# A RetNet recurrence with a low-rank mixer on one core: three pieces of the hand-written order moved

## The chip, the core and the metric

The kernel runs on one core of a Trainium2 chip. A core has five engines that work through their own queues in order and meet through semaphores: PE (matrix products; PEld is its weight load), DVE (vector), ACT (scalar activations and copies), POOL (GpSimd) and SP (which here only issues DMAs). PE writes its results to PSUM, which has eight banks of 128 partitions x 2 KB; DVE and ACT read them from there into SBUF, the working memory. The metric is the device time of one execution in microseconds (us), as the median of several runs. All times inside an execution are counted from the start of the profiled span.

## The reference

```python
def _attn_ref(q, k, v):                        # 4 batches, 8 heads, 768 steps, 64
    gamma = 1.0 - 2.0 ** (-5.0 - np.arange(H)); scale = 1.0 / np.sqrt(D)
    for t in range(S):
        state = gamma * state + np.einsum('bhd,bhe->bhde', k[:, :, t], v[:, :, t])
        y[:, :, t] = scale * np.einsum('bhd,bhde->bhe', q[:, :, t], state)

def _moe_ref(x, U, V, w_ch1, w_ch2):           # x: 4 x 768 x 512, rank 32, hidden 2048
    h = x.transpose(0, 2, 1) @ U @ V
    u = x + h.transpose(0, 2, 1)
    ch = np.maximum(u @ w_ch1, 0.0) @ w_ch2
    return u + ch
```

The heads' outputs y are laid side by side as x (768 x 512 for each batch). A low-rank mix over the 768 steps makes u from x; a two-layer perceptron with a relu is added to it.

## The kernel before

**Stages.** The recurrence is computed in chunks of 128 steps, six for each batch. For a chunk `ci`, `state` (L482) adds the product of the chunk's k and v to a running state in PSUM bank `st` (L490) and has ACT copy it out (L498); `score` (L501) multiplies k with q (L506); `screen` (L510) has DVE multiply the two score banks with the causal mask (L516), giving `a0` and `a1`; `mix` (L532) forms the chunk's x from the state (L540) and from `a0` and then `a1` with v (L545) in bank `o`, which ACT copies out. q and k have to be turned first. In batch 1 that is done on PE (`turn_pe`, L461: four or eight 128x128 transposes, L465, into bank `qk`), with ACT copying the bank out, q in another order of columns (`q_order`, L453). In batches 2 and 3 DMA transposes do it (L475), and DVE reorders q (L87).

**From x to u.** `lr_proj` (L559) multiplies x with U into bank `o` (L563) and DVE copies the result `pc`. `lr_grow` (L571) multiplies `pc` with V (L576); the 512 columns are spread over four banks, in the order s, s, o and a last one, which is st here. `lr_add` (L580) has DVE add one of these banks to x, in place (L582). This is "plain u": rows are steps. `lr_turn` (L599) then turns u by DMA into `uT` for the perceptron. In batch 1, uT is made on PE instead (`x_turn`, `grow_turned`), and plain u comes later, when the perceptron of batch 1 already runs, since it is needed only for the final sums.

**The perceptron.** `mlp_pieces(b)` lists the pieces of batch b: 32 `up` pieces of four products (L763; 16 of 512 columns, 16 of 256), each emptied by ACT (L773) or DVE (L771) with a relu into `gT`; then the second layer. For batch 0 that is six output rows of 16 products of 512 columns in pieces of four (`down`, L814), each row ended by a DVE sum (L819). For batches 1 to 3 a seven-product scheme is used on 2x2 blocks (`down_pairs`, L643): each of the 21 pieces p1 to p7 of blocks 0 to 2 is a chain of eight products of 256 columns (L655) into banks called A (two of them), B and C. Several pieces add into one bank in turn, and between them DVE reads the bank: `keep` (L665) makes the sums `da`, `db`, `dc` (L668), `give` (L674) parts of the output rows (L676). The next piece on that bank has to wait for the read. `order` (L747) is the list of pieces. The scheme needs sums of the weights (`w2_sums`, L623) and of `gT` (`g_sums`, L633), all DVE instructions of line L608.

**What sets the order.** The program is in the order in which Python emits it; there is no scheduler. `weave` (L828) walks through the perceptron's pieces of batch b-1 and puts the recurrence of batch b between them. Each track is a list of steps with a start and an end as fractions of the pieces' summed cost; a step is emitted ahead of the first piece that begins at or after its mark. So a mark moves a step only in whole pieces, and steps with marks between the same two pieces are emitted in order of their marks. All five engines' queues follow from it: what a step issues to DVE stands ahead of everything that later steps issue to DVE, whether it is ready or not.

**The marks of this change.** In the block for b = 1 (perceptron of batch 0), `at` (L948) and `lag` place the steps of the six chunks; `more` and `late_by` (L1004, L1005) shift the score and the mix of each. L958 to L963 place the transposes, L970 to L973 the twelve weight sums. In the block for b = 2 (perceptron of batch 1), L984 to L986 place the growth and the four adds of batch 1's plain u; `two` (L978) places pairs of chunks, L1009 the last two mixes of batch 2. `t` (L1022) and the offsets at L1033 to L1041 place the projection, growth, adds and turns of batches 2 and 3.

PSUM banks are given out by `bank` from rings (L69): mlp has banks 0 to 2 (and bank 6 as a fourth from b = 2 on), s 3 and 4, o 5, qk 6, st 7, A 6 and 0, B 1, C 2. Whoever takes a bank again waits until its last reader is done.

Of the kernel before, what the change touches and what calls it, by code (L numbers as in the profile page):

```python
# [18 lines left out]
def kernel(  # L19
# [19 lines left out]
    NCB = DM // P  # L39
# [71 lines left out]
    def pair(b, sc):  # L111
        i = 2 * sc
        qs = [("q", b, sc, hh) for hh in range(2)]
        if b == 1:
            return [("k", b, i), *qs, ("v", b, i), ("k", b, i + 1),
                    ("v", b, i + 1)]
        return [("k", b, i), ("k", b, i + 1), *qs, ("v", b, i),
                ("v", b, i + 1)]
# [131 lines left out]
    for i in range(NST):  # L250
        t = consts.tile([P, 4, P], bf16, name=f"state{i}")
# [201 lines left out]
    def q_order(b, sc, src):  # L453
        t = rmid.tile([P, 2, 4, P], bf16, tag="qO", bufs=2, name=f"qO_{b}_{sc}")
        dst = t.rearrange("p x n (m two) -> p two n x m", two=2)
        src = src.rearrange("p two n (x m) -> p two n x m", x=2)
        for two in range(2):
            evac("A" if b == 1 else "D", dst[:, two], src[:, two])
        live["qO", b, sc] = t
# [147 lines left out]
    def part(f, *args, **kw):  # L607
        return lambda: f(*args, **kw)  # L608
# [14 lines left out]
    def w2_sums(m):  # L623
        r = ds(m, 2)
        lo, hi = w2b[:, r], w2b[:, ds(m + NH, 2)]
        b11, b12, b21, b22 = (lo[..., :DQ], lo[..., DQ:], hi[..., :DQ],
                              hi[..., DQ:])
        t1, t2, t3, t4 = (t[:, r] for t in w2t)
        return [part(nc.vector.tensor_tensor, o, x, y, ALU.subtract)
                for o, x, y in ((t1, b12, b11), (t2, b22, t1),  # L630
                                (t3, b22, b12), (t4, b21, t2))]
# [303 lines left out]
    for b in range(1, B + 1):  # L935
        tracks = []
        if b > 1:
            old = b - 1 < SEVEN
            first = [part(lr_expand, b - 1, 4, 2, "qk" if old else "st"),
                     part(lr_turn_pe, b - 1, 4, "qk" if old else "o")  # L940
                     if b < 3 else part(lr_turn, b - 1, 4)]
            if not old:
                RINGS["mlp"] = [6, 0, 1, 2]
        tracks.append((first, *((0.02, 0.2), (0.02, 0.14), (0.0, 0.06),
                                (0.0, 0.03))[b - 1]))
        if b < B:
            if b == 1:
                at = [0.503, 0.61, 0.675, 0.735, 0.793, 0.845]  # L948
                lag = [0.01, 0.035, 0.065]
                for sc in range(NSC):  # L950
                    keys = pair(b, sc)
                    c0, c1 = 2 * sc, 2 * sc + 1
                    if sc:
                        tracks.append(([part(prep_keys, b, keys[:AHEAD])],
                                       at[c0] - 0.1, 1))
                    tracks.append(([part(prep_keys, b, keys[AHEAD:])],
                                   at[c1] - 0.1, 1))
                    for f, d in ((part(turn_pe, "q", b, sc),  # L958
                                  at[c0] + (0.015, -0.042, -0.042)[sc]),
                                 (part(turn_pe, "k", b, sc, (0,)),  # L960
                                  at[c0]),
                                 (part(turn_pe, "k", b, sc, (1,)), at[c1])):
                        tracks.append(([f], d, d))  # L963
                for sc in range(NSC):
                    tracks.append(([part(prep_keys, 2, pair(2, sc))],
                                   0.752 + 0.03 * sc, 1))
                for i in range(2 * NSC):
                    tracks.append(([part(turn_dma, "kq"[i % 2], 2, i // 2)],
                                   0.84, 0.84))
                for f, d in zip(w2_sums(0) + w2_sums(2) + w2_sums(4),  # L970
                                (0.515, 0.535, 0.575, 0.6, 0.655, 0.67, 0.72,
                                 0.735, 0.78, 0.8, 0.875, 0.895)):
                    tracks.append(([f], d, d))  # L973
            else:
                at = [(0.205, 0.06)[b - 2] + (0.074, 0.1)[b - 2] * i
                      for i in range(NCK)]
                lag = [0.0, 0.04, 0.1]
                two = [(0.25, 0.395, 0.595), (0.1, 0.27, 0.44)][b - 2]  # L978
                if b == 2:
                    for _ in range(RING):  # L980
                        feed_one(False)
                    steps = [(0.01 + 0.022 * i, f)
                             for i, f in enumerate(w2_sums(6))]
                    steps.append((0.125, part(lr_grow, 1, 0, 4, "st")))  # L984
                    steps += [(0.125 + 0.022 * c, part(lr_add, 1, 0, 4, (c,)))
                              for c in range(NCB)]  # L986
                    for sc in range(NSC):
                        steps.append((0.57 + 0.08 * sc,
                                      part(prep_keys, 3, pair(3, sc))))
                        for nm in "kq":  # L990
                            if not sc:
                                steps.append((0.64, part(turn_dma, nm, 3, sc)))
                else:
                    steps = [(0.08, part(turn_dma, nm, 3, sc))
                             for sc in (1, 2) for nm in "kq"]
                for d, f in steps:
                    tracks.append(([f], d, d))
            if b > 1:
                for sc in range(NSC):
                    d = two[sc] - (0.04, 0.05, 0.08 if b == 2 else 0.05)[sc]  # L1000
                    tracks.append(([lambda b=b, sc=sc: q_order(
                        b, sc, live["q", b, sc])], d, d))
            for i in range(NCK):
                more = (0.012, 0.0, 0.0, 0.0, 0.0, -0.015)[i]  # L1004
                late_by = (0.015, 0.0, 0.012, 0.0, 0.01, 0.0)[i]  # L1005
                if b == 2 and i > 3:
                    p = two[2] + 0.05 * (i - 4)
                    steps = [(state, p - 0.035), (score_one, p),
                             (mix, p + (0.075, 0.067)[i - 4])]  # L1009
                elif b > 1:  # L1010
                    p = two[i // 2]
                    steps = [(state, p + (-0.035, 0.02)[i % 2]),
                             (mix, p + (0.08, 0.12)[i % 2])]
                    if i % 2 == 0:
                        steps.append((score_two, p))
                else:
                    steps = [(state, at[i] + lag[0]),
                             (score_one, at[i] + lag[1] + more),
                             (mix, at[i] + lag[2] + late_by)]
                for f, d in steps:  # L1020
                    tracks.append(([part(f, b, i)], d, d))
            t = at[-1] + lag[2] if b == 1 else two[-1] + 0.122  # L1022
            if b == 1:
                turns = [part(x_turn, c, j0, b, tag)
                         for c, tag in enumerate(("qk", "st", "s", "s"))
                         for j0 in (0, 2)]
                for fs, d in ((turns[:4], t + 0.006),
                              ([part(lr_open, b), part(lr_proj, b)], t + 0.022),
                              (turns[4:], t + 0.023),
                              ([part(grow_turned, b)], t + 0.044)):  # L1030
                    tracks.append((fs, d, d))
            else:
                for fs, d in (([part(lr_open, b), part(lr_proj, b)],  # L1033
                                0.025),
                              ([part(lr_grow, b, 0, 4, "st")], 0.047),
                              ([part(lr_add, b, 0, 4, (0,))], 0.047),
                              ([part(lr_add, b, 0, 4, (1,))], 0.057),
                              ([part(lr_add, b, 0, 4, (2,))], 0.082),
                              ([part(lr_add, b, 0, 4, (3,))], 0.102),
                              ([part(lr_turn, b, 0)], 0.107),  # L1040
                              ([part(lr_turn, b, 2)], 0.108)):  # L1041
                    tracks.append((fs, t + d, t + d))
        weave(b == 1, mlp_pieces(b - 1), *tracks)

# [28 lines left out]
```

## Time and profile before

| | |
|---|---|
| median of 7 runs | 221.83 us (221.64 to 222.46) |
| the profiled execution | 222.58 us |
| its span, first to last instruction | 220.8 us |
| granted PE clock | 1.000 |
| ACT L773, 98 relu evacuations | 47.4 us busy |
| DVE L771, 30 relu evacuations | 16.7 us busy |
| DVE L516, 128x512 masks | 682 ns each |
| PE L763, 512 products | 88.6 us busy |
| PE L655, chains of eight 256-column products | 273 ns for one product, pipelined |

The times of a PE instruction overlap: a product's duration runs until its result has left the array, and the next one begins earlier. So PE's pace is read from start to start. In the timeline, each line is: start, time in us, engine, line, operation, output<-inputs, shape, how many instructions are merged, and in brackets how long the engine had been idle and what it then waited for.

The stretches that matter here: from 51 to 59 us the first chunk of batch 1 runs between the last `up` pieces and the first `down` pieces of batch 0; from 84 to 96 us the perceptron of batch 1 starts and batch 1's plain u is made; from 116 to 127 us the last chunk of batch 2 and its u are made among the p pieces of batch 1.

### The profile page before, as it was taken

How to read it: one execution, taken by the hardware profiler on the slowest of the kernel's cores; microseconds unless marked ns; L12 is line 12 of the kernel's file. 1: busy time of each engine (PE TensorE's matmuls, PEld its weight loads, DVE VectorE, ACT ScalarE, POOL GpSimd, SP SyncE). 2: the span in 40 equal slices, each digit the busy share in tenths (PEclk: the TensorE clock that was granted, in tenths of full speed). 3: DMA queues.
4: the chain of work that ended last, by engine and by line, in shares of the span. 5: the costliest groups of instructions: out<-in, count | busy, mean ns of one | idle time of the engine just before them, and what ended most of it. 6: DMA issues, size and time to landing. Idle time of an engine off the chain costs nothing. (4 is left out here: it accounts for less than half of the span.)

```text
span 220.8 us, 5521 instructions
## 1 busy us (share of the span) xinstructions
PE 212.9 (96%) x2239; PEld 148.0 (67%) x2239; DVE 143.0 (65%) x303; ACT 92.8 (42%) x192; POOL 81.5 (37%) x121
## 2 busy tenths in 40 slices
PE   7979999999999999999999999999999999999994
PEld 2668754486456554567788784767788856668884
DVE  7487764433648748698785846598986442867443
ACT  3337845457355514667822005768510035551000
POOL 5439698897787957000049930000000000000000
PEclk9999999999999999999999999999999999999999
DMA  5999999999999999999999467900006341000043
GB/s 171 300 293 301 290 355 275 348 354 243 232 225 221 247 221 204 139 339 249 237 227 185 167 144 187 149 0 4 0 3 145 119 143 23 3 1 0 11 158 119
DMA packets 84489, 38.82 MB, mean 176 GB/s; under 512 B 58384, under 2 KB 77552, under 8 KB 84464
## 3 DMA queue, kind: packets, MB, share of 16 engines
q1 hardware_dynamic: 83456, 36.84, 69.8%
q10 hardware_dynamic: 1008, 1.64, 2.0%
q8 instruction: 17, 0.28, 0.5%
q14 instruction: 8, 0.07, 0.1%
HBM read 27.46 MB, written 6.29 MB: 153 GB/s over the span
## 5 line engine op out<-in xcount | busy, mean ns | idle before, releaser
L763 PE MATMUL mlp<-uT,w1b 128*128 128x512 f16 (+1 forms) x512 | 88.6, 326 | 0.0
L773 ACT ACTIVATE gT<-mlp 128x512 f16<-128x512 f32 (+1 forms) x98 | 47.4, 490 | 63.4 <-PE mlp L763 61.2
L763 PEld LDWEIGHTS <-w1b 128*128 128x128 f16 x512 | 48.2, 98 | 30.0 <-POOL w1b L340 0.2
L771 DVE TENSOR_SCALAR gT<-mlp 128x512 f16<-128x512 f32 (+1 forms) x30 | 16.7, 556 | 25.7 <-PE mlp L763 25.3
L655 PEld LDWEIGHTS <-gT 128*128 128x128 f16 x288 | 27.7, 98 | 3.3
L814 PE MATMUL mlp<-w2b,gT 128*128 128x512 f16 x96 | 23.6, 380 | 0.0
L516 DVE TENSOR_TENSOR a<-s,mask 128x512 bf16<-128x512 f32 x26 | 16.7, 682 | 10.0 <-PE s L506 10.0
L306 POOL TENSOR_TENSOR kd<-in,gk 128x512 bf16<-128x512 f32 x18 | 19.3, 1083 | 6.4 <-DMA in<-in_k_dram 6.3
L655 PEld LDWEIGHTS <-gS 128*128 128x128 f16 x200 | 19.2, 98 | 3.1 <-issue 0.5
L306 POOL TENSOR_TENSOR qd<-in,gq 128x512 bf16<-128x512 f32 x18 | 18.4, 1045 | 0.0
L655 PE MATMUL A<-w2t,gT 128*128 128x256 f16 x144 | 18.4, 273 | 0.0
L85 ACT ACTIVATE state<-st 64x256 bf16<-64x256 f32 x40 | 15.0, 374 | 6.7 <-PE st L386 3.2
L85 ACT ACTIVATE x<-o 128x512 f16<-128x512 f32 x20 | 11.9, 595 | 13.9 <-PE o L545 13.5
L814 PEld LDWEIGHTS <-gT 128*128 128x128 f16 x96 | 8.4, 98 | 8.1 <-issue 0.2
L304 POOL CAST vd<-in 128x512 bf16<-128x512 f32 x18 | 11.6, 662 | 1.6 <-DMA in<-in_v_dram 0.9
L346 POOL CAST w2b<-in 128x512 f16<-128x512 f32 x16 | 9.8, 616 | 1.5 <-DMA in<-in_moe_w_ch_dram 0.8
L608 POOL COPY gate<-gT 128x1 f16<-128x1 f16 x1 | 0.2, 190 | 26.5 <-DVE gT L608 26.5
L582 DVE TENSOR_TENSOR x<-s,x 128x256 f16<-128x256 f32 (+1 forms) x16 | 8.1, 548 | 2.7 <-PE st L576 1.5
L340 POOL CAST w1b<-in 128x512 f16<-128x512 f32 x16 | 9.2, 618 | 0.4 <-DMA in<-in_moe_w_ch_dram 0.2
L655 PE MATMUL B<-w2b,gT 128*128 128x256 f16 x72 | 9.3, 273 | 0.0
L655 PE MATMUL A<-w2t,gS 128*128 128x256 f16 x72 | 9.0, 273 | 0.3 <-DVE da L668 0.3
L655 PE MATMUL A<-w2b,gT 128*128 128x256 f16 x72 | 8.8, 273 | 0.0
(156 smaller groups left out, 292.8 us busy)
## 6 DMA issues: line engine op xcount, KB each, us to landing
in<-in_moe_w_ch_dram SPq DMA_DIRECT2D x32, 256.0 KB, 5.4
in<-in_k_dram SPq DMA_DIRECT2D x24, 256.0 KB, 5.4
in<-in_q_dram SPq DMA_DIRECT2D x24, 256.0 KB, 5.0
in<-in_v_dram SPq DMA_DIRECT2D x24, 256.0 KB, 5.4
out_dram<-o SPq DMA_DIRECT2D x16, 256.0 KB, 2.0
out_dram<-o ACTq DMA_DIRECT2D x6, 256.0 KB, 2.0
out_dram<-o SPq DMA_DIRECT2D x3, 128.0 KB, 1.7
Uf<-in_moe_U_dram SPq DMA_DIRECT2D x1, 96.0 KB, 5.4
```

The costliest lines, as they stand in the source:

```text
L85: nc.scalar.activation(dst, src, AF.Copy)
L304: nc.gpsimd.tensor_copy(out=t, in_=src)
L306: nc.gpsimd.tensor_tensor(t, src, g, op=ALU.mult)
L340: nc.gpsimd.tensor_copy(out=w1b[:, c, ts(mb, 512)], in_=take("w1", mb, c))
L346: nc.gpsimd.tensor_copy(out=w2b[:, m], in_=take("w2", m))
L516: nc.vector.tensor_tensor(a, four(sp[i]), causal(mask), op=ALU.mult)
L582: nc.vector.tensor_tensor(us[b][:, ds(j0, nj), ts(c, P)], four(grown[b][c])[:, :nj], xs[b][:, ds(j0, nj), ts(c, P)], op=ALU.add)
L655: nc.tensor.matmul(acc[key, i], lhs[:, m, ts(i, P)], rhs[:, m], start=(fresh and m == 0), stop=(m == NH - 1), skip_group_check=True)
L763: nc.tensor.matmul(g_p[:, :sz], w1b[:, c, ts(m, P)], uTs[b][:, ds(j, nj), c], start=(c == 0), stop=(c == NCB - 1))
L771: nc.vector.tensor_relu(gT[:, m, ds(lo, sz)], g_p[:, :sz])
L773: nc.scalar.activation(gT[:, m, ds(lo, sz)], g_p[:, :sz], AF.Relu)
L814: nc.tensor.matmul(ch, gT[:, m, ts(j, P)], w2b[:, m], start=(m == 0), stop=(m == NM - 1))
```

## The change

Only marks move, and the order of the four adds of batch 1.

```diff
@@ b == 1: transposes of q @@
                     for f, d in ((part(turn_pe, "q", b, sc),
-                                  at[c0] + (0.015, -0.042, -0.042)[sc]),
+                                  at[c0] + (0.035, -0.042, -0.042)[sc]),
@@ b == 1: weight sums @@
                 for f, d in zip(w2_sums(0) + w2_sums(2) + w2_sums(4),
-                                (0.515, 0.535, 0.575, 0.6, 0.655, 0.67, 0.72,
+                                (0.51, 0.525, 0.54, 0.585, 0.655, 0.67, 0.72,
                                  0.735, 0.78, 0.8, 0.875, 0.895)):
@@ b == 2: batch 1's plain u @@
                     steps.append((0.125, part(lr_grow, 1, 0, 4, "st")))
-                    steps += [(0.125 + 0.022 * c, part(lr_add, 1, 0, 4, (c,)))
-                              for c in range(NCB)]
+                    steps += [(0.125 + 0.022 * i, part(lr_add, 1, 0, 4, (c,)))
+                              for i, c in enumerate((3, 2, 0, 1))]
@@ the chunks' steps @@
-                more = (0.012, 0.0, 0.0, 0.0, 0.0, -0.015)[i]
-                late_by = (0.015, 0.0, 0.012, 0.0, 0.01, 0.0)[i]
+                more = (0.027, 0.0, 0.0, 0.0, 0.0, -0.015)[i]
+                late_by = (0.032, 0.0, 0.012, 0.0, 0.01, 0.0)[i]
                 if b == 2 and i > 3:
                     p = two[2] + 0.05 * (i - 4)
                     steps = [(state, p - 0.035), (score_one, p),
-                             (mix, p + (0.075, 0.067)[i - 4])]
+                             (mix, p + (0.07, 0.047)[i - 4])]
@@ the end of batches 2 and 3 @@
-            t = at[-1] + lag[2] if b == 1 else two[-1] + 0.122
+            t = at[-1] + lag[2] if b == 1 else two[-1] + (0.102, 0.122)[b - 2]
...
                               ([part(lr_add, b, 0, 4, (0,))], 0.047),
-                              ([part(lr_add, b, 0, 4, (1,))], 0.057),
-                              ([part(lr_add, b, 0, 4, (2,))], 0.082),
-                              ([part(lr_add, b, 0, 4, (3,))], 0.102),
-                              ([part(lr_turn, b, 0)], 0.107),
-                              ([part(lr_turn, b, 2)], 0.108)):
+                              ([part(lr_add, b, 0, 4, (1,))], 0.052),
+                              ([part(lr_add, b, 0, 4, (2,))], 0.066),
+                              ([part(lr_add, b, 0, 4, (3,))], 0.076),
+                              ([part(lr_turn, b, 0)], 0.08),
+                              ([part(lr_turn, b, 2)], 0.081)):
```

What the two programs' queues say, instruction by instruction:

- Chunk 0 of batch 1 on PE. Before: 4 products of output row 0, k transposes, state, q transposes, 8 products of row 0, scores, the last 4 of row 0, mix, 8 products of row 1. After: 4 of row 0, k transposes, state, 4 of row 0, q transposes, the last 8 of row 0, scores, 4 of row 1, mix, 4 of row 1. On DVE, the third weight sum and row 0's L819 come before the two masks and not behind them; the fourth weight sum stays behind.
- Batch 1's plain u on DVE. Before: banks s, s, a relu evacuation, o, st. After: st, o, the relu evacuation, s, s. PE's queue is the same.
- The end of batch 2 on PE. Before: p7 of block 1, p2 of block 1, mix of chunk 5, p4 of block 0, projection, p3 of block 0, growth, p4 of block 1. After: p7 of block 1, mix of chunk 5, p2 of block 1, projection, p4 of block 0, growth, p3 of block 0, p4 of block 1. On DVE, the adds of banks o and st come before the two reads of p4 and p5 of block 1 and not behind them, and the read of p3 of block 0 comes between the second and the third add.
- The end of batch 3: the marks change, and the order on every queue is as before. ACT, POOL and SP have the same order throughout.

## The prediction

> **What bounds the kernel now.** I read the page's busy times first, then who waited for whom on PE, then the timeline around each PE wait. All times are us from the span's start.
>
> ```profile
> PE 212.9 (96%) x2239; PEld 148.0 (67%) x2239; DVE 143.0 (65%) x303; ACT 92.8 (42%) x192; POOL 81.5 (37%) x121
> ```
>
> ```profile
> PE qk L465 <- ACT kT L85: 0.5, 1, 0.5
> ...
> PE st L490 <- DVE x L582: 0.3, 1, 0.3
> PE o L545 <- DVE a L516: 0.3, 1, 0.3
> PE A L655 <- DVE da L668: 0.3, 1, 0.3
> ```
>
> The first fence is the page's row of busy times, the second PE's waits (total, times, longest). PE is the bound, and the granted clock is full (1.000). After the start-up four single PE waits are left. Their idle figures count from a modelled end of the last matmul, so I measure by starts instead. PE's own pace, start to start, is 0.217 for a 128x512 product, 0.109 for a 128x256 one (eight: 0.87), 0.22 for four 128x128 and 0.23 for the eight 128x64 of a mix.
>
> ```profile
> 52.20 0.39 PE L465 MATMUL qk<-ident,kd 128*128 128x128 bf16 x4
> 52.43 0.39 PE L490 MATMUL st<-vd,kd 128*128 128x128 bf16 x4
> ...
> 52.63 0.60 ACT L85 ACTIVATE kT<-qk 128x512 bf16<-128x512 bf16 x1 [0.70 <-PE qk L465]
> ...
> 53.28 0.61 PE L465 MATMUL qk<-ident,qd 128*128 128x128 bf16 x8 [0.46 <-ACT kT L85]
> ...
> 55.54 0.40 PE L506 MATMUL s<-qO,kT 64*128 64x128 bf16 x8
> ...
> 55.97 1.29 DVE L516 TENSOR_TENSOR a<-s,mask 128x512 bf16<-128x512 f32 x2 [3.38 <-PE s L506]
> ...
> 57.18 0.68 DVE L819 TENSOR_TENSOR o<-mlp,x 128x512 f32<-128x512 f32 x1
> ...
> 57.32 0.29 PE L545 MATMUL o<-vd,a 128*128 128x64 bf16 x4 [0.29 <-DVE a L516]
> ```
>
> Chunk 0 of batch 1. After the L490 group (52.43+0.22=52.65) PE stands until ACT has emptied bank qk: 53.28, a gap of 0.63. The mix's first half starts at 56.74; its second half would follow 0.12 later, at 56.86, but the second mask is done at 57.26 and it starts at 57.32: 0.46.
>
> ```profile
> 90.45 1.29 DVE L582 TENSOR_TENSOR x<-s,x 128x512 f16<-128x512 f32 x2 [1.47 <-PE st L576]
> ...
> 93.50 0.68 DVE L582 TENSOR_TENSOR x<-st,x 128x512 f16<-128x512 f32 x1
> ...
> 94.32 0.38 PE L490 MATMUL st<-vd,kd 128*128 128x128 bf16 x4 [0.32 <-DVE x L582]
> ```
>
> Start of batch 2. The products begun at 90.35 (8 of 512, 16 of 256 columns: 3.48) are issued by 93.83; the state product waits for bank st, whose add is the fourth: gap 0.49.
>
> ```profile
> 123.13 1.28 DVE L582 TENSOR_TENSOR x<-s,x 128x512 f16<-128x512 f32 x2
> ...
> 125.92 0.68 DVE L582 TENSOR_TENSOR x<-st,x 128x512 f16<-128x512 f32 x1
> 126.52 0.41 DVE L668 TENSOR_TENSOR da<-A,x 128x256 f32<-128x256 f32 x1
> ...
> ...
> 126.98 1.03 PE L655 MATMUL A<-w2t,gS 128*128 128x256 f16 x8 [0.29 <-DVE da L668]
> ```
>
> End of batch 2. Two of batch 2's adds stand ahead of the sum da; p6 of block 2 goes on adding into that bank, so it waits: p2 began at 125.65, 0.87 later is 126.52, it starts at 126.98: 0.46. The four gaps make 2.04.
>
> **The change part by part.** No instruction is added or removed; pieces move. Lags I use, all from the timeline: 0.05 to 0.06 from an evacuation's end to the PE work it frees (53.23 to 53.28, 57.26 to 57.32); 0.43 from a score group's start to its first mask (55.54 to 55.97); 1.07 from the start of the last four 512-column products, or of eight 256-column ones, to DVE's read (72.30 to 73.37; 120.29 to 121.36). DVE issues 128x512 operations from PSUM every 0.60 and 128x256 ones every 0.34.
>
> *Chunk 0.* Four of output row 0's L814 products move ahead of the q transposes, so these come at 52.65+0.87=53.52, past the 53.28 that ACT allows: 0.63 saved. All remaining eight products of row 0 now come before the scores. ACT's reordered q starts 0.64 after the transposes (53.28 to 53.92), so at 54.16, takes 1.34 and ends at 55.50; the scores come at 53.52+0.44+1.73+0.10 (the switch to 64 rows)=55.79, so that wait stays hidden, by 0.24. But row 0 is now complete before the scores, and its L819 stands ahead of the masks on DVE. It starts 1.07 after its last four products (54.83): 55.90. The scores can be masked from 55.79+0.43=56.22; DVE comes to them at 56.50, and the masks end at 57.18 and 57.79. PE has four products of row 1 after the scores (55.79+0.33+0.87=56.99), then waits to 57.24 for the first mask and, 0.12 further, to 57.85 for the second: 0.25+0.49=0.74 where 0.46 was. Net saving 1.09-0.74, about 0.34: check, 57.97 plus the four products left (0.87) is 58.84, and the next k transposes started at 59.17. Behind these waits nothing else stands on PE but row 1; the two other weight differences (L608) and the x evacuation have slack of over a microsecond.
>
> One thing is not shown: the third L608 moves from 57.78 to about 52.55, beside POOL's key product (52.85 to 53.89). L608 takes 0.41 alone and took 1.26 at 58.11, over POOL's product from 57.87 to 59.09. At 1.26 it ends at 53.81, 2.1 before L819 needs DVE, so I take nothing. The other end: held through POOL's run, which pauses at 55.90, it delays L819 by 0.34 and chunk 0 saves 0. If L819 didn't hold the masks at all, it saves 1.09. The Trainium skill (SBUF — State Buffer, "Who interferes with whom") speaks against this move: a VectorE instruction with two SBUF inputs and a GpSimd one that reads SBUF shut each other out entirely, whichever comes second. The 1.26 agrees in kind; by the rule's worst order the sum would be 0.34 smaller, by the row it is unchanged, since L608 starts before POOL's product.
>
> *Batch 1's adds in batch 2.* The order is st, o, s, s: the st add is done at 90.45+0.69=91.14, so the state product starts at 93.83: 0.49 saved. The two s adds go to 92.90 and 93.50, the relu at 94.09 stays; the s banks are wanted by scores only after 95.46. From here PE is 0.49 early against a DVE that has no idle time between 92.29 and 102.87. Three places decide. The q reorder (94.42+0.79=95.21, PE may go at 95.27) before scores at 95.95-0.49=95.46: covered by 0.19. The masks (97.82+1.28=99.10) before the mix at 99.76-0.49=99.27: covered by 0.11. The next q reorder (102.08+0.79=102.87, so 102.93) before scores at 103.38-0.49=102.89: 0.04 lost. At 103.05 and 103.92 DVE itself waited for PE (0.18, 0.45), so it follows from there. Net 0.45. Ends: 0.49, and 0 if DVE's run slips by the whole.
>
> *Batch 2's end.* The mix of chunk 5 goes ahead of p2 of block 1; projection, growth and adds move one product earlier. Mix 5 at 118.96 needs bank o, emptied at 118.28+0.60=118.88, so 118.93: covered by 0.03. p2 at 119.41; its evacuation of x takes ACT from 119.62 to 120.22, the projection comes at 119.41+0.87+0.10=120.38: covered. p4 of block 0 at 120.84 (0.46 as in 121.25 to 121.71); growth at 120.84+0.87+0.10=121.81, with the projection's copy done at 120.96+0.29=121.25. p3 of block 0 at 122.14, p4 of block 1 at 123.01, p5 at 123.88. On DVE: p4's read at 121.91, adds s at 122.25 and 122.86, p3's read from 123.46 to 123.88, adds o and st at 123.80 and 124.41, p4's and p5's reads at 125.01 and 125.35, da at 124.80+1.07=125.87 to 126.29. p5 of block 1 reuses bank C, which p3's read frees at 123.88+0.05: a new wait of 0.05. p6 comes at 126.55, its da is done: 0.46 saved. Net 0.41; ends 0.46, and 0 if the read of C came another 0.4 later. The two uT transposes on SP, issued at 126.75 after the last add, go out near 125.2 in the same place of SP's queue; they land 3.2 after issue and are wanted at 132.5, so that gains nothing. Batch 3's new marks leave every queue's order as it was: 0.
>
> Sum: 0.34+0.45+0.41=1.20. The profiled execution took 222.58 (span 220.80 and 1.78 around it): 221.38 by this sum. The median of the runs is 221.83, 0.75 below the profiled one; the waits are the same instructions in both, so 220.63.
>
> **The rivals.** (1) All four gaps go: 2.04 less, 219.79. For it: each named releaser does finish earlier or PE comes later. Against: L819 now stands ahead of the masks. (2) Chunk 0 gives its whole saving back, because DVE reaches L819 0.34 late: 0.86 less, 220.97. For it: L608 was drawn out threefold beside POOL; against: two microseconds of slack. (3) In batch 2, too, the early PE runs into the full DVE and loses it at the masks and q reorder (margins 0.11 and 0.19, one already short), and chunk 0 gives nothing: 0.41 less, 221.42, which is no difference here. (4) Slower: L608 stays shut out by POOL beyond its run, through the pause at 55.90 and the cast at 56.78 to 57.39, and L819, the masks and the mix with it. Each 0.1 that L819 starts after 56.24 costs 0.1 of the other 0.86, so it is slower once L819 starts after 57.10. L608 let in at 57.39 only, and L819 0.33 behind it (57.78 to 58.11) at 57.72: 0.62 over, 222.45. Against: POOL stands idle for 0.89 before that cast.
>
> **How the numbers follow.** This kernel's runs tell 0.2% (0.44) from nothing. Forecast 0.60, at 220.63; (1) 0.08; (2) 0.17; (3) 0.10; (4) 0.05. Faster: forecast, (1) and (2): 0.85; same 0.10; slower 0.05. The range goes from the forecast with some of chunk 0's second wait gone (0.4 more: 220.2) to rival (2) with a quarter of a microsecond lost at the thin margins of batch 2 (221.25).
>
> **What would show it.** In the changed profile: no wait of L465 for kT; the L819 of row 0 starting just before the first masks, and both halves of the first mix waiting (0.25 and 0.49 by starts); L490 after the growth without a wait, and the next two scores at most 0.05 late; p6 of block 2 without a wait, p5 of block 1 up to 0.1 late. I am wrong if a wait of over 0.3 appears that is not listed here.

## The result, and the profile after

The changed kernel takes 220.60 us (median of 12 runs, 219.93 to 221.13) where the kernel before takes 221.86 us (31 runs): a ratio of 0.9938, with a 95% interval from 0.9924 to 0.9952, so 1.26 us or 0.6% less. The profiled execution took 221.05 us, its span is 219.3 us (220.8 before).

PE's waits after the change, from the view of who waited for whom (total, times, longest):

```profile
PE mlp L189 <- DVE ones L181: 1.5, 1, 1.5
PE s L404 <- ACT qT L85: 1.4, 2, 0.8
PE s L404 <- DVE a L413: 0.4, 1, 0.4
PE o L545 <- DVE a L516: 0.3, 1, 0.3
```

The first three lie in the start-up, in batch 0. Of the four waits of before, the one of L465, the one of L490 and the one of L655 are gone; the one of L545 is still listed. The timeline shows what became of each. Chunk 0 of batch 1:

```profile
51.10 1.03 PE L814 MATMUL mlp<-w2b,gT 128*128 128x512 f16 x4
...
53.27 0.61 PE L465 MATMUL qk<-ident,qd 128*128 128x128 bf16 x8
...
55.54 0.40 PE L506 MATMUL s<-qO,kT 64*128 64x128 bf16 x8
...
55.65 0.69 DVE L819 TENSOR_TENSOR o<-mlp,x 128x512 f32<-128x512 f32 x1 [3.38 <-PE mlp L814]
...
56.26 1.28 DVE L516 TENSOR_TENSOR a<-s,mask 128x512 bf16<-128x512 f32 x2
...
56.99 0.17 PEld L545 LDWEIGHTS <-a 128*128 128x128 bf16 x4 [0.57 <-DVE a L516]
56.99 0.29 PE L545 MATMUL o<-vd,a 128*128 128x64 bf16 x4
...
57.59 0.29 PE L545 MATMUL o<-vd,a 128*128 128x64 bf16 x4 [0.31 <-DVE a L516]
...
58.58 0.39 PE L465 MATMUL qk<-ident,kd 128*128 128x128 bf16 x4
```

The same two ends of the stretch in the kernel before:

```profile
51.34 1.03 PE L814 MATMUL mlp<-w2b,gT 128*128 128x512 f16 x4
...
59.17 0.39 PE L465 MATMUL qk<-ident,kd 128*128 128x128 bf16 x4
```

L814 starts at 51.10 where it started at 51.34: 0.24 come from the start-up and are not the change's (see the last section). The k transposes that began at 59.17 begin at 58.58, 0.59 earlier: chunk 0 gives 0.35. L819 runs ahead of the two masks, and both halves of the mix wait. The view of waits lists only the second; the first shows at the weight load, which stood idle until the mask was done. Four products after the scores PE would be free at 55.54+0.33+0.87=56.74 and goes on at 56.99 (0.25); 0.12 later the second half would follow and starts at 57.59 (0.48).

The start of batch 2:

```profile
89.88 0.69 DVE L582 TENSOR_TENSOR x<-st,x 128x512 f16<-128x512 f32 x1 [1.07 <-PE st L576]
...
93.25 0.39 PE L490 MATMUL st<-vd,kd 128*128 128x128 bf16 x4
...
102.42 0.21 PE L506 MATMUL mlp<-qO,kT 64*128 64x128 bf16 x1
102.46 0.21 PE L506 MATMUL o<-qO,kT 64*128 64x128 bf16 x1
...
103.00 1.04 PE L763 MATMUL mlp<-uT,w1b 128*128 128x512 f16 x4
```

In the kernel before, the last of these lines is:

```profile
104.07 1.04 PE L763 MATMUL mlp<-uT,w1b 128*128 128x512 f16 x4
```

The bank's add is done at 90.57, the state product starts without a wait: 94.32 to 93.25, 1.07 earlier, 0.48 more than at 58.58. Products after the scores of chunk 3 began at 104.07 and begin at 103.00: 1.07 still, nothing given back.

The end of batch 2:

```profile
122.38 0.41 DVE L676 TENSOR_TENSOR o<-C,db 128x256 f32<-128x256 f32 x1
...
122.85 1.03 PE L655 MATMUL C<-w2t,gS 128*128 128x256 f16 x8
...
124.59 1.04 PE L655 MATMUL B<-w2b,gT 128*128 128x256 f16 x8
...
124.79 0.42 DVE L668 TENSOR_TENSOR da<-A,x 128x256 f32<-128x256 f32 x1
...
125.46 1.04 PE L655 MATMUL A<-w2t,gS 128*128 128x256 f16 x8
```

The sum da is done at 125.21, p6 of block 2 starts 0.87 after p2 (124.59), without a wait: 126.98 to 125.46, 1.52 earlier, 0.44 more than at 103.00. To the last product it stays at 1.51. So the three parts give 0.35+0.48+0.44=1.27.

### The profile page after: what moved, and what is told of

Same layout as the page of the kernel before. It is cut to its first block, busy times and chain, and to the rows that moved or that the text cites. A ratio compares the mean times of both kernels' runs of the same rounds, so it can differ in the third digit from the quotient of the medians.

```text
span 219.3 us, 5522 instructions
## 1 busy us (share of the span) xinstructions
PE 212.6 (97%) x2239; PEld 148.0 (67%) x2239; DVE 143.0 (65%) x303; ACT 92.8 (42%) x192; POOL 82.0 (37%) x121
## 4 chain that ended last, share of the span: by engine, by line
PE 92%; DVE 3%; ACT 3%; issue 1%; ACTq 0%
PE mlp L763 38%; PE A L655 15%; PE mlp L814 9%; PE C L655 6%; PE B L655 4%; PE mlp L189 3%; PE o L545 2%; PE s L506 2%; ACT qT L85 2%; PE o L540 1%; PE st L490 1%; PE qk L465 1%; PE mlp L363 1%; PE s L576 1%; DVE a L413 1%; PE mlp L193 1%
## 5 line engine op out<-in xcount | busy, mean ns | idle before, releaser
L655 PEld LDWEIGHTS <-gT 128*128 128x128 f16 x288 | 27.7, 98 | 3.3
L814 PE MATMUL mlp<-w2b,gT 128*128 128x512 f16 x96 | 23.7, 380 | 0.0
L655 PEld LDWEIGHTS <-gS 128*128 128x128 f16 x200 | 19.2, 98 | 2.6
L306 POOL TENSOR_TENSOR qd<-in,gq 128x512 bf16<-128x512 f32 x18 | 19.6, 1111 | 0.8 <-DMA in<-in_q_dram 0.8
L655 PE MATMUL A<-w2t,gT 128*128 128x256 f16 x144 | 18.4, 273 | 0.0
L85 ACT ACTIVATE state<-st 64x256 bf16<-64x256 f32 x40 | 15.0, 374 | 6.2 <-PE st L386 3.2
L85 ACT ACTIVATE x<-o 128x512 f16<-128x512 f32 x20 | 11.9, 596 | 13.3 <-PE o L545 12.9
L814 PEld LDWEIGHTS <-gT 128*128 128x128 f16 x96 | 8.4, 98 | 7.8 <-issue 0.2
L304 POOL CAST vd<-in 128x512 bf16<-128x512 f32 x18 | 10.9, 616 | 2.1 <-DMA in<-in_v_dram 1.7
L655 PE MATMUL B<-w2b,gT 128*128 128x256 f16 x72 | 9.3, 273 | 0.0
L608 POOL COPY gate<-gT 128x1 f16<-128x1 f16 x1 | 0.2, 192 | 23.8 <-DVE gT L608 23.8
L655 PE MATMUL A<-w2t,gS 128*128 128x256 f16 x72 | 9.0, 273 | 0.0
L655 PE MATMUL A<-w2b,gT 128*128 128x256 f16 x72 | 8.8, 273 | 0.0
```

What stands on the lines that cost most here:

```text
L85: nc.scalar.activation(dst, src, AF.Copy)
L304: nc.gpsimd.tensor_copy(out=t, in_=src)
L306: nc.gpsimd.tensor_tensor(t, src, g, op=ALU.mult)
L655: nc.tensor.matmul(acc[key, i], lhs[:, m, ts(i, P)], rhs[:, m], start=(fresh and m == 0), stop=(m == NH - 1), skip_group_check=True)
L814: nc.tensor.matmul(ch, gT[:, m, ts(j, P)], w2b[:, m], start=(m == 0), stop=(m == NM - 1))
```

## The experiments

The table gives PE's start of the same product in each kernel less that in the kernel before, in us, at five places of the program (times of before); each comes from one profile. A difference between two neighbouring columns is what that stretch gained. The last four kernels of the table ran once each, so only their traces are read and no times are given.

| kernel | 50 us | 61 us | 96 us | 112 us | 132 us |
|---|---|---|---|---|---|
| the changed kernel | -0.24 | -0.59 | -1.07 | -1.07 | -1.51 |
| chunk0_alone | -0.08 | -0.43 | -0.43 | -0.43 | -0.43 |
| adds_alone | -1.12 | -1.12 | -1.61 | -1.61 | -1.60 |
| end2_alone | -0.67 | -0.67 | -0.67 | -0.67 | -1.11 |
| mix0_later | -0.08 | -1.17 | -1.65 | -1.65 | -2.09 |
| masks_first | -0.64 | -1.26 | -1.74 | -1.74 | -2.18 |
| q_turn_only | -0.68 | -0.69 | -0.69 | -0.68 | -0.68 |
| st_third | -0.47 | -0.82 | -1.30 | -1.30 | -1.74 |
| adds2_only | -1.20 | -1.20 | -1.20 | -1.20 | -1.52 |

**Chunk 0's marks alone.** The four marks of `turn_pe` q, `w2_sums`, `more` and `late_by` of the change, nothing else.

```diff
-                                  at[c0] + (0.015, -0.042, -0.042)[sc]),
+                                  at[c0] + (0.035, -0.042, -0.042)[sc]),
-                (0.515, 0.535, 0.575, 0.6, 0.655, 0.67, 0.72,
+                (0.51, 0.525, 0.54, 0.585, 0.655, 0.67, 0.72,
-                more = (0.012, 0.0, 0.0, 0.0, 0.0, -0.015)[i]
-                late_by = (0.015, 0.0, 0.012, 0.0, 0.01, 0.0)[i]
+                more = (0.027, 0.0, 0.0, 0.0, 0.0, -0.015)[i]
+                late_by = (0.032, 0.0, 0.012, 0.0, 0.01, 0.0)[i]
```

> Only the marks of batch 1's chunk 0 are changed. Theory (three gains that add, because PE is the bound and every stretch after a gain follows PE): PE's wait of 0.63 us ahead of the q transposes is gone, the first mix waits 0.25 us for its first mask and 0.49 for its second (0.46 for the second alone before); all that follows comes 0.34 us earlier; the time about 0.34 us less, 0.15 %. Rival 2 (the gain given back through a late L819): L819 starts after the masks could have started by 0.6 us or more, the shift is 0. Rival 3 (the gain lost later in batch 1, where POOL or the DMAs set the pace): 0.34 us at 59 us, and less of it at 84 us.

0.35 us are gained between 50 and 61 us, and they are still whole at 132 us, so rivals 2 and 3 are out for this part. The time is 221.61 us against 221.78, a ratio of 0.9992 (0.9974 to 1.0009): by itself the part is too small for the timed runs, and only the trace shows it.

**The order of batch 1's adds alone.**

```diff
-                    steps += [(0.125 + 0.022 * c, part(lr_add, 1, 0, 4, (c,)))
-                              for c in range(NCB)]
+                    steps += [(0.125 + 0.022 * i, part(lr_add, 1, 0, 4, (c,)))
+                              for i, c in enumerate((3, 2, 0, 1))]
```

> Only the order of batch 1's four plain adds is changed (st, o, s, s). Theory: the state product after the growth starts 0.49 us earlier, at 93.83 us, and about 0.45 us is kept; the scores near 102.9 us come after their q reorder by 0.04 us. Time 0.45 us less, 0.2 %. Rival 3 (the vector engine is full from 92.3 to 102.9 us and takes the gain back): the 0.49 us are there at 94 us, and 0.1 or less of them at 104 us.

0.48 us are gained at 96 us and none is lost at 112 us. Time 221.43 us, ratio 0.9980 (0.9965 to 0.9995).

**The end of batch 2 alone.**

```diff
-                             (mix, p + (0.075, 0.067)[i - 4])]
+                             (mix, p + (0.07, 0.047)[i - 4])]
-            t = at[-1] + lag[2] if b == 1 else two[-1] + 0.122
+            t = at[-1] + lag[2] if b == 1 else two[-1] + (0.102, 0.122)[b - 2]
...
```

> Only the end of batch 2 is changed (last mix one product chain earlier, projection, growth and the adds with it). Theory: p6 of block 2 no longer waits for da; p5 of block 1 waits 0.05 us at most for bank C; what follows comes 0.41 us earlier, and so does the end. Time 0.41 us less, 0.2 %. Rival: the earlier last mix waits for bank o (copied out only 0.03 us before it), or p5 for bank C, and the shift is below 0.2 us.

0.44 us are gained. Time 221.42 us, ratio 0.9988 (0.9973 to 1.0002). The three ratios together make 0.40% less, the change 0.62%; with intervals of 0.15% to either side on each part this is no contradiction and no proof. The traces add up: 0.35+0.48+0.44 for the parts, 1.27 for the whole.

**The first mix one piece later**, on top of the change.

```diff
-                late_by = (0.032, 0.0, 0.012, 0.0, 0.01, 0.0)[i]
+                late_by = (0.042, 0.0, 0.012, 0.0, 0.01, 0.0)[i]
```

> The changed kernel, and the first mix of batch 1 one piece later still (0.042 where the change has 0.032): eight products of row 1 and the next k transposes stand between the scores and the mix, not four. Theory: the two waits of the first mix (0.25 and 0.47 us by starts) are covered and nothing else waits, since the q transposes behind it need ACT's copy of the k transposes, done 0.5 us before they are reached: 0.72 us less than the changed kernel, 219.9 us. Rival: ACT's queue (copy of k, then of x, then of the state) becomes late in its turn and the q transposes or the next scores wait: gain below 0.3 us.

From its timeline:

```profile
56.03 1.90 PE L814 MATMUL mlp<-w2b,gT 128*128 128x512 f16 x8
...
57.77 0.39 PE L465 MATMUL qk<-ident,kd 128*128 128x128 bf16 x4
57.99 0.40 PE L545 MATMUL o<-vd,a 128*128 128x64 bf16 x8
...
59.31 0.61 PE L465 MATMUL qk<-ident,qd 128*128 128x128 bf16 x8
```

Eight products and the k transposes now stand between scores and mix, and the eight products of the mix run as one group; the q transposes come 1.54 us after the k transposes, with no wait listed. The stretch gains 1.09 us where the change gains 0.35, 0.74 more. The time is 219.93 us against 221.78, ratio 0.9916 (0.9898 to 0.9935), the fastest version here. It ran once more:

> The changed kernel with the first mix one piece later, again. Theory: 0.9910 of the kernel before, within 0.0015, and below the changed kernel by 0.6 to 0.8 us.

220.01 us against 221.52, ratio 0.9914 (0.9890 to 0.9937), again 1.09 us in chunk 0's stretch. The changed kernel has 0.9938 (0.9924 to 0.9952). The intervals overlap a little, so the 0.7 us between the two rests on the traces, which show it in the same place both times.

**The masks ahead of row 0's sum**, on top of the change: the L819 of row 0 is emitted after the masks of chunk 0.

```diff
+                    def end():
+                        nc.vector.tensor_tensor(o_sb, ch, us[b][:, j],
+                                                op=ALU.add)
-                    nc.vector.tensor_tensor(o_sb, ch, us[b][:, j], op=ALU.add)
+                    if j == 0:
+                        owed.append(end)
+                    else:
+                        end()
...
     def score_one(b, ci):
         score(b, ci)
         screen(b, ci)
+        while owed:
+            owed.pop(0)()
```

> The changed kernel with row 0's sum (L819 there, three or four lines further down here) put on the vector engine's queue behind the two masks of chunk 0 and not ahead of them; all else as in the changed kernel. Theory (the sum ahead of the masks makes the first half's wait): the masks start 0.43 us after the scores, the first half of the first mix does not wait, the second waits about 0.45 us as it did before the change: 0.27 us less than the changed kernel up to 61 us. Rival (the mix waits because one piece between scores and mix is too little for two masks, whatever stands ahead): both waits stay, 0.25 and 0.47 us.

In its timeline (L548 is the mix, L823 the sum, L611 the weight sums here):

```profile
55.58 1.29 DVE L516 TENSOR_TENSOR a<-s,mask 128x512 bf16<-128x512 f32 x2 [2.62 <-PE s L506]
...
56.35 0.28 PE L548 MATMUL o<-vd,a 128*128 128x64 bf16 x4
56.79 0.68 DVE L823 TENSOR_TENSOR o<-mlp,x 128x512 f32<-128x512 f32 x1
56.92 0.29 PE L548 MATMUL o<-vd,a 128*128 128x64 bf16 x4 [0.29 <-DVE a L516]
```

The masks start 0.43 after the scores (55.15), the first half no longer waits, the second waits as before the change. The stretch gains 0.62, 0.27 more than the change, as expected. So L819 ahead of the masks costs 0.27, and the rest of the mix's wait, 0.46, is the second mask itself.

**Only the q transposes later.** The first two lines of chunk 0's diff, with `more` and `late_by` as before.

> The kernel before, with only the q transposes of chunk 0 one piece later and the third weight sum earlier; scores and mix stay where they were. Theory (a wait covered by moving one step comes back at the next step that depends on it): no wait of the q transposes on ACT, but the scores, now four products behind them, wait for ACT's reordered q until 55.55 us where PE is there at 54.93: 0.62 us; the second mask's wait stays 0.46; chunk 0 gains 0 within 0.05 us. Rival (the first wait was the whole matter): 0.6 us gained at 61 us.

```profile
54.87 0.40 PE L506 MATMUL s<-qO,kT 64*128 64x128 bf16 x8 [0.56 <-ACT qO L85]
```

The wait went from the q transposes to the scores; by starts it is 0.62 there (the four products begun at 53.29 end at 54.16, and 0.10 is the switch to 64 rows). Chunk 0 gains 0.01. It needs both moves: the later transposes open the space and the later scores use it.

**st as the third add**, on top of the change.

```diff
-                              for i, c in enumerate((3, 2, 0, 1))]
+                              for i, c in enumerate((0, 1, 3, 2))]
```

> The changed kernel with batch 1's plain adds in the order s, s, st, o. Theory (a due time decides, not who is first): the st add is the third, runs right after the relu at 92.9 us (by the clock of the kernel before) and ends 0.25 us before the state product needs the bank; the 0.48 us gained there stay whole. Rival (the bank must be emptied first, or the later adds push the next relu and q reorder back): the state product waits again, or less than 0.3 us are left at 104 us.

```profile
92.08 0.68 DVE L582 TENSOR_TENSOR x<-st,x 128x512 f16<-128x512 f32 x1
...
93.02 0.39 PE L490 MATMUL st<-vd,kd 128*128 128x128 bf16 x4
```

The add ends 0.26 before the state product starts, and the same 0.48 us are gained and kept. Exchanging the two adds behind the relu is enough.

**Only batch 2's adds closer together**, with the mix, the projection and the growth where they were.

```diff
-                              ([part(lr_add, b, 0, 4, (1,))], 0.057),
-                              ([part(lr_add, b, 0, 4, (2,))], 0.082),
-                              ([part(lr_add, b, 0, 4, (3,))], 0.102),
-                              ([part(lr_turn, b, 0)], 0.107),
-                              ([part(lr_turn, b, 2)], 0.108)):
+                              ([part(lr_add, b, 0, 4, (1,))], 0.052),
+                              ([part(lr_add, b, 0, 4, (2,))], 0.066),
+                              ([part(lr_add, b, 0, 4, (3,))], 0.076),
+                              ([part(lr_turn, b, 0)], 0.08),
+                              ([part(lr_turn, b, 2)], 0.081)):
```

> The kernel before, with only batch 2's adds closer together (offsets of the adds and turns), the last mix, the projection and the growth left where they were. Theory (da is late because of the adds ahead of it on the vector engine): the last two adds now stand ahead of the reads of p4 and p5 of block 1 partly, da ends about 0.3 us sooner, p6 of block 2 waits 0.16 us and not 0.46: 0.30 us gained. Rival (what gains is that projection and growth come one product chain earlier): p6 waits 0.46 us as before.

```profile
124.99 0.41 DVE L668 TENSOR_TENSOR da<-A,x 128x256 f32<-128x256 f32 x1
125.46 1.03 PE L655 MATMUL A<-w2t,gS 128*128 128x256 f16 x8
```

p6 starts 0.06 after da's end and 1.00 after p2 (124.46): it waits 0.13, and 0.32 is gained. So most of the gain at the end of batch 2 is DVE's order. The other 0.12 is put down by difference to the earlier mix, projection and growth; no run moves them alone. But this kernel loses some 0.17 again at the start of batch 2's perceptron: its first product begins 0.40 after the growth (130.79 to 131.19), 0.22 in the kernel before (132.31 to 132.53). The transposes of uT fit as the cause: the second goes out at 126.22 and took 4.8 us to land, so near 131.05, 0.14 before the product starts. The trace names no releaser for this wait, so that is an inference.

## Why the prediction was right

The time, 220.60 us, is that of the forecast (220.63). That the two agree to 0.03 is luck: the interval of the ratio alone leaves 0.3 us to either side. What carries the account is that the sum holds part by part, in the places and for the waits that were named: 0.34, 0.45 and 0.41 were worked out, 0.35, 0.48 and 0.44 were measured.

- *Chunk 0.* The wait for ACT's copy went, the scores' wait for the reordered q stayed hidden, and L819 ahead of the masks made the new wait: 0.25 and 0.49 were expected, 0.25 and 0.48 came. Rival (1), that nothing takes the place of the four gaps, fell at this point; masks_first takes one share of the new wait away (0.27), mix0_later all of it (0.74).
- *The third L608 beside POOL.* Taken at nothing, rightly, for the reason given, two microseconds of slack. In the changed kernel's profile it came at 51.85, before POOL's product (52.03), and took 0.41. In masks_first (L611 there) it came second and took 1.27, much as in the worst row of before (1.26): POOL's product ran from 51.58 to 52.68, the weight sum from 51.69 to 52.96. It still ended 2.6 us ahead of the masks. Rivals (2) and (4) needed more than that. This agrees with the Trainium skill (SBUF — State Buffer, "Who interferes with whom"), that the second of two such instructions is shut out until the first ends.
- *Batch 1's adds.* 0.48 is the whole gap. The step that was off is the 0.04 lost at the second q reorder. The first of these scores did come late, by 0.11 (102.31 would have been the undisturbed start, 102.42 it was, 0.15 after the reorder's end at 102.27; the trace names no releaser). But the next score product writes bank o, and before the change it had started 0.16 after the first, just behind ACT's copy of x into which that bank is emptied:

  ```profile
  102.89 0.59 ACT L85 ACTIVATE x<-o 128x512 f16<-128x512 f32 x1
  ...
  103.38 0.23 PE L506 MATMUL mlp<-qO,kT 64*128 64x128 bf16 x1
  ...
  103.54 0.21 PE L506 MATMUL o<-qO,kT 64*128 64x128 bf16 x1
  ```

  After the change this copy ends at 102.41 and that product starts at 102.46, 1.07 earlier like all the rest: its wait took the delay in, and the group ended in step. The prediction had not reckoned with that wait. Rival (3) fell: the two other thin margins, 0.19 and 0.11, held.
- *The end of batch 2.* The new wait of p5 for bank C was 0.02, not 0.05 (122.85, where p4's start of 121.96 plus 0.87 makes 122.83), hence 0.44 for 0.41. (The prediction's own starts, 126.55 against 126.98, already gave 0.43.)
- *uT.* It gains nothing, as said, but not with the landing time that was used. 3.2 us was the kernel before's; issued 2.6 us earlier on the clock, the two took 5.0 and 4.3. The second went out at 125.47, so it landed near 129.75, 1.27 before its first product at 131.02. In the kernel before it went out at 128.08 and landed near 131.24, 1.29 before 132.53. With 3.2 us this cover, the time between landing and use, would have grown to 2.35; it stayed as it was, and in adds2_only it all but went.

## What to carry to other kernels

Where one engine is the bound and its waits are few, a prediction can be made wait by wait: find each gap by start times, move it, and follow every queue behind the moved step until the engine that lost its cover is idle of itself again. A wait that is covered at one step turns up at the next step that needs the same data unless that one moves as well; whoever is emitted first on a queue holds up what is due sooner, and being early enough counts, not being first. A transfer that starts earlier may also land more slowly (here 3.8 to 5.7 us for 3.1 to 3.3), so its old duration is no safe cover.

## What the runs showed that was not expected

The program is the same up to 50 us in all these kernels, and yet PE reaches that point between 0.03 us (mix0_later_again) and 1.20 us (adds2_only) sooner than in the profile of before; most of it arises in the first 18 us, around the first transposed blocks and scores, and three of the ten give 0.10 to 0.24 of it back between 20 and 25 us. From 30 us on, the untouched stretches agree to within 0.02 us from kernel to kernel. So a single span can be off by a microsecond here, which is the size of the whole change, while the difference between two places of the trace can be trusted to some hundredths. What makes the start-up vary was not looked into.

The landing of batch 2's uT takes a different time when it is issued earlier. Issued at the old place it took 3.1 to 3.3 us (the kernel before, chunk0_alone, adds_alone, q_turn_only); issued earlier, with the end of batch 2 changed, 3.8 to 5.7 (the other seven profiles). The view of the issuing line, in the kernel before and in the changed one:

```profile
DMA to landing us min/median/max: 3.2/3.2/3.3
```

```profile
DMA to landing us min/median/max: 4.3/4.6/5.0
```

What it meets on the DMA engines was not settled. Between 122 and 126 us they are busier in the changed kernel, at shares of 1.31 and 1.06 in the windows view where the kernel before has 0.54 and 0.36; but in adds2_only, where the two took 4.1 and 4.8 us, the shares there are 0.47 and 0.03. What all seven slow profiles have in common is a store of an output row, issued on ACT's queue between the two transposes, as in the changed kernel:

```profile
124.14 1.23 SPq L600 DMA_TRANSPOSE uT<-x  x1
...
124.68 0.37 ACTq L615 DMA_DIRECT2D out_dram<-o  x1
...
125.47 1.90 SPq L600 DMA_TRANSPOSE uT<-x  x1
```

In the four others it goes out 1.3 us ahead of the first (125.44 against 126.75 in the kernel before), and it lands in 2.0 to 2.1 us there, in 3.2 to 5.0 in the seven. No run moves the store alone, so it is a lead and not a shown cause.
